# Moving background work, one scatter and 24 transposes in a fused attention, expert and dense kernel

## Chip, core and metric

The kernel runs on one core of a Trainium2 chip. The metric is device time in microseconds (us): the median of three runs of the kernel before is 793.03 us (792.22 to 793.25). The core has TensorE (PE: matmuls, and PEld: its weight loads), VectorE (DVE), ScalarE (ACT), GpSimd (POOL) and SyncE (SP), which issues most transfers. Each engine works through its own instructions in the order in which the program gives them.

## The reference

Attention over a window of 128 with a bias by distance, an expert layer that sends each token to its best of 8 experts, and a dense layer with a squared ReLU. What follows concerns the end of the expert layer and the dense layer.

```python
def reference(**kwargs):
    attn_out = _attn_ref(q, k, v)                      # 4 x 8 x 576 x 64
    x = attn_out.transpose(0, 2, 1, 3).reshape(2304, 512)
    # expert layer: e = argmax of the logits of a token
    #   out = gate * (relu(x @ w1[e]) @ w2[e])         # 512 -> 1024 -> 512
    x = _moe_ref(x=x, **moe_kwargs)
    h = x @ w_in                                       # 512 -> 2048
    r = np.maximum(h, 0.0)
    g = r * r
    return (g @ w_out).astype(np.float32)              # 2048 -> 512
```

All matmuls that matter are done in pairs of numbers: a value is split into a high half and the rest (the low half), and high x high, high x low and low x high are added up. A split is a cast on ScalarE (high) and a subtraction on VectorE or GpSimd (low).

## The kernel before

**Expert stage (up to L1080).** Tokens are gathered into five slots, four of 512 and a last one of 384 (three tiles of 128). A slot has eight up products (`ffn1`, split by `relu_split`) and then, tile by tile, 24 matmuls down (`ffn2`), an eviction and a scatter of the tile's rows to the buffer `yd` in DRAM (`put`: a ScalarE copy and `scatter`, an indirect DMA on GpSimd). In the last slot the third tile is left over. Behind the slots stands a loop (`tc.For_i`, L1106) for tokens that found no slot; its number of turns is read at run time, and in the run shown it is none. After it, `yload(0)` loads the rows of the first dense block on SyncE (it has to wait for the scatters into `yd`), the last slot's third tile is computed, and the rows of the first block are turned so that features lie on partitions: eight groups of three 128x128 pieces, each a matmul with the identity, onto which two 384-column matmuls add what the third tile brings (L1346 to L1353).

**Dense stage.** The hidden features are cut into 4 passes (`PASSES`), the tokens into 3 blocks of 768 (`NB`): 12 visits (`visits`), back and forth over the blocks. A visit has a way up and a way down. `way_up` is a fast matrix product with seven products instead of eight; I number them 1 to 7. A product has two halves of six matmuls of 384 columns. The PSUM banks are three pairs: products 1, 3, 5 and 7 add into the first pair, 2 and 6 into the second, 4 has the third. Between them ScalarE copies the results of products 1 to 3 out (L1263), and VectorE adds those to the results of products 4 to 6 (L1266) and squares them (L1242). So product 3 can't start before the copy of product 1, product 5 not before that of product 3, and product 7 not before VectorE's adds of product 5. `squared` and `split_late` make the halves: a cast on ScalarE (L1234), the low half on GpSimd (L1235). `way_down` has six tiles: the first half of tiles 3, 4, 5, the second half of the same with their eviction (`down_end`, VectorE L1302 from the second pass on, then a store to `ya` on SyncE), and tiles 0, 1, 2 whole. While a visit runs, SyncE loads the next block's operands (`reload`, 768 KB after each product) and earlier sums (`down_load`).

**Background work.** `bg` is a list of generators, and `tick` runs the next step of the first of them. Ticks are called in `way_up` and `way_down` (and in the last expert slot); the instructions of a step enter the queues of their engines there. Three kinds of work run so:
- `weights(p)` (L794): loads two tiles of w_in for pass p, makes four sums (GpSimd) and seven splits of 512 columns, loads two tiles of w_out and splits them (1024 columns). It has 17 steps; the load of w_out is the tenth. `weights(0)` runs in the last expert slot, `weights(1)` from the third visit of pass 0 on, `weights(p+1)` from the second visit of passes 1 and 2 on.
- `late_convs` (L783): four conversions of 64-bit weights, from the first visit of passes 1 and 2 on, in six steps each: load (512 KB); nothing; a ScalarE multiply (L635) and a VectorE mask (L636); a VectorE step (L638); another (L640); a VectorE step (L642) and a GpSimd add (L643). The next step stores the result and issues the next conversion's load.
- `prepare` (operands of the next block) is stepped by itself and is not changed.

Of the kernel before, what the change touches and what calls it, by code (L numbers as in the profile page):

```python
# [24 lines left out]
NSLOT = 5  # L25
MAXSLOT = 12
SHORT = 384
# [25 lines left out]
def attention_moe_kernel(ctx, tc, qh, kh, v, mid, wg, mb, w1, w2, win, wout, out):  # L53
# [740 lines left out]
    def weights(p):  # L794
# [15 lines left out]

        top, low = load(2 * p), load(2 * p + 1)
        yield
        yield
        yield
        yield
        a11, a12, a21, a22 = top[:, :512], top[:, 512:], low[:, :512], low[:, 512:]
        split("a11", a11)
# [10 lines left out]
        s4 = both(a12, s2, ALU.subtract)  # L828
        split("s2", s2)
        yield  # L830
        r = [load(2 * p + 8 + i) for i in range(2)]
        split("a22", a22)
        yield
        split("s4", s4)
        yield
        yield
        for i in range(2):
            h, l = wt("left", F32R), wt("left", F32R)
# [195 lines left out]
    for s in range(NSLOT):  # L1034
# [33 lines left out]
        for i in range(n // 128):  # L1068
            advance_load(8 * s + 4 + i + LA + 1)
            if not nxt and i == n // 128 - 1:  # L1070
                break
            c = slice(128 * i, 128 * i + 128)
            ps = bank("t")
            for f in range(8):
                ffn2(ps, hs[f][0][:, c], hs[f][1][:, c], W[s, 4 + f // 2], f, f == 0, f == 7)
                if f == 4 and 128 * i < nn and nxt:
                    turn(s + 1, i, xr[s + 1][1][i], "v", nn)
                if f == 1 or f == 5:
                    flush()
                    conv_pace(16 * s + 8 + 2 * i + f // 4)  # L1080
                if not nxt and f % 2 == 0:
                    tick()
            put(s, i, ps)
            advance_split(8 * s + 4 + i + LA + (0 if nxt else 1))

    conv_step(EARLY + 1)
# [4 lines left out]
    for s in range(NSLOT - 1):  # L1091
        del xr[s]
        for j in range(8):
            del W[s, j]
    p = ps = None
    held.append({})

# [33 lines left out]
        put("d", 0, ps)  # L1131
    held.clear()
    del xr["d"], xT["d"]
    yload(0)

    s, i = NSLOT - 1, SHORT // 128 - 1
    ids, hot = sm.tile([128, 1], F32, tag="ids", name="ids", bufs=1), wt("left", F32R)
    dve.tensor_copy(ids, xr[s][0][:, i:i + 1])  # L1138
    dve.tensor_tensor(ids, ids, again, op=ALU.add)
# [110 lines left out]
    def way_up(p, ahead, after):  # L1250
# [3 lines left out]
        for n, (o, wo, ps, first) in enumerate((("b11", "a11", a, True), ("t1", "s1", x, True), ("t2", "s2", a, False), ("b21", "a12", z, True), ("t3", "s3", a, False), ("b22", "s4", x, False), ("t4", "a22", a, False))):  # L1254
# [3 lines left out]
            for q in range(2):  # L1258
# [8 lines left out]
                    squared((n == 4, q, n != 3), c)  # L1267
                else:
                    squared((True, q, False), part(), ps[q])
                if q or p == 0:  # L1270
                    tick()
            after(n)
        split_late()

# [36 lines left out]
    def way_down(j, p, between):  # L1311
# [9 lines left out]
        for n, i in enumerate((3, 4, 5)):  # L1321
            ps[i] = bank("vvt"[n])
            products(i, [(True, 0), (True, 1)], True, False)
            tick()
        for i in (3, 4, 5):
            products(i, [(False, 0), (False, 1)], False, True)
            down_end(j, p, i, ps[i])
            between()
            tick()
        for n, i in enumerate((0, 1, 2)):  # L1330
            ps[i] = bank("tvv"[n])
            products(i, [(False, 0), (False, 1), (True, 0), (True, 1)], True, True)
            down_end(j, p, i, ps[i])
            between()
            tick()
        gs.clear()

    def step(n):
# [7 lines left out]
    for n, (k, h) in enumerate(((0, 0), (0, 1), (1, 1), (1, 0))):  # L1346
        for c in range(2):
            p = bank("xmssvvxm"[2 * n + c])[:, :HT]
            m = slice(128 * (2 * k + c), 128 * (2 * k + c) + 128)
            for r in range(3):  # L1350
                pe.matmul(p[:, 128 * r:128 * r + 128], yrow(0, 3 * h + r)[:, m], ident, start=r == 0, stop=False, skip_group_check=True)
            passes(p, [(yhl[:, 512 * b_ + m.start:512 * b_ + m.stop], hot[:, HT * h:HT * h + HT]) for b_ in range(2)], False, True, skip_group_check=True)
            act.copy(raw[k, h][:, c, :], p)  # L1353
        step((2, 1, 3, 1)[n])
# [4 lines left out]
    for n_, (p, j) in enumerate(visits):  # L1359
# [12 lines left out]
            if kept:  # L1372
                reload(visits[n_ + 1][1], n)

        if n_ % NB == (1 if p else 2) and p + 1 < PASSES:
            bg.append(weights(p + 1))
        if n_ % NB == 0 and 0 < p < PASSES - 1:
            bg.append(late_convs(EARLY + LATE * (p - 1)))
        way_up(p, ahead, after)
        between = lambda: None  # L1380
        if fresh is not None:
# [57 lines left out]
```

## Time and profile before

| what | value |
| --- | --- |
| median of three runs | 793.03 us |
| the profiled execution | 790.08 us, span 788.4 us |
| TensorE busy (matmuls) | 744.9 us, 94% of the span |
| TensorE weight loads | 636.0 us, 81% |
| VectorE, ScalarE, GpSimd | 504.0, 342.6, 300.8 us |
| granted clock of TensorE, mean | 0.987 |
| DMA | 174.72 MB, 222 GB/s |

TensorE is busy nearly throughout, so what is read below is where it is not, where its clock is lower, and which engine ends each such wait. The expert stage ends at about 360 us, the dense stage runs from 381.6 us to the end. In a row of the timeline stand: start, length (us), engine, line, operation, output<-inputs, shapes, the number of instructions run together, and in brackets the idle time before the first of them with what ended it. "SPq" and the like are issues of transfers.

### The profile page before, as it was taken

Reading aid. Unit: us, or ns where it says so; the run is one execution under the profiler, and the core shown is the slowest. Engines: PE = TensorE matmul, PEld = TensorE weight load, DVE = VectorE, ACT = ScalarE, POOL = GpSimd, SP = SyncE. Lnnn points to the kernel's source line nnn. Section 1 sums busy time; section 2 is a strip of 40 time slices with the busy share of each in tenths; the row PEclk is TensorE's granted clock in tenths of the full one; section 3 lists DMA queues with packets and bytes.
Section 4 is the critical chain, followed back from the end, with each engine's and each line's share of the span. In section 5 each row is a group of like instructions: output and inputs, shape, how many; then the busy total and the mean of one; then the engine's idle time right before and its main releaser. Section 6 shows DMA issues by size and latency. Waiting matters only on the chain.

```text
span 788.4 us, 12648 instructions
## 1 busy us (share of the span) xinstructions
PE 744.9 (94%) x4207; PEld 636.0 (81%) x4207; DVE 504.0 (64%) x1274; ACT 342.6 (43%) x833; POOL 300.8 (38%) x322
## 2 busy tenths in 40 slices
PE   9999987999999999997989979999999999999997
PEld 7777766777888888895969767978989789898896
DVE  7788889789677768591655436447575475642542
ACT  6676675236345444460655735314332243331230
POOL 4322355022642533441334425235452363540431
PEclk9999999999999999998999997999999999999999
DMA  8567440349776976733668471779827898286832
GB/s 273 172 223 221 141 168 27 121 135 347 241 266 215 319 231 234 267 137 108 228 243 343 183 284 41 291 274 341 303 102 295 277 359 293 95 301 229 338 120 81
DMA packets 71155, 174.72 MB, mean 222 GB/s; under 512 B 10032, under 2 KB 18480, under 8 KB 71088
## 3 DMA queue, kind: packets, MB, share of 16 engines
q1 hardware_dynamic: 68048, 163.93, 58.4%
q0 software_dynamic: 3040, 9.96, 3.3%
q8 instruction: 34, 0.56, 0.3%
q14 instruction: 33, 0.27, 0.1%
HBM read 117.76 MB, written 56.10 MB: 221 GB/s over the span
## 4 chain that ended last, share of the span: by engine, by line
PE 39%; DMA 5%; DVE 4%; issue 3%; POOL 2%; ACT 1%; SPq 0%; POOLq 0%; DVEq 0%; ACTq 0%
PE v L691 14%; PE t L691 10%; PE s L691 9%; PE x L691 2%; PE m L691 2%; DMA w<-wout 2%; DMA w<-win 1%; DVE cr L1242 1%; POOL row L643 1%; DVE cr L1266 1%; DMA w<-wc 1%; POOL hd L1235 1%; DVE w L803 1%; DMA yd<-row,idx 0%; DMA wc<-row 0%
## 5 line engine op out<-in xcount | busy, mean ns | idle before, releaser
L1235 POOL TENSOR_TENSOR hd<-cr,hd 128x384 fp32r<-128x384 f32 x96 | 119.1, 1267 | 144.8 <-ACT hd L1234 137.3
L691 PE MATMUL v<-w,hd 128*128 128x512 f32 x576 | 141.3, 395 | 5.3 <-POOL hd L1235 2.7
L691 PEld LDWEIGHTS v<-w,hd 128*128 128x128 f32 x576 | 107.9, 189 | 32.0 <-POOL hd L1235 6.1
L691 PE MATMUL s<-xq,w 128*128 128x384 f32 x576 | 111.1, 340 | 8.0 <-DVE cr L1266 6.2
L691 PEld LDWEIGHTS s<-xq,w 128*128 128x128 f32 x576 | 102.2, 191 | 11.0 <-DVE cr L1266 7.0
L691 PE MATMUL t<-w,h 128*128 128x512 f32 x408 | 100.6, 400 | 5.6 <-DVE ids L1138 5.6
L691 PEld LDWEIGHTS t<-w,h 128*128 128x128 f32 x408 | 76.3, 191 | 22.2 <-issue 6.0
L643 POOL TENSOR_TENSOR row<-row 128x512 int32<-128x512 int32 x32 | 46.9, 1465 | 117.4 <-DVE row L642 80.2
L1234 ACT CAST hd<-cr 128x384 fp32r<-128x384 f32 x96 | 49.1, 513 | 72.4 <-DVE cr L1242 67.0
L691 PE MATMUL t<-w,hd 128*128 128x512 f32 x288 | 69.2, 389 | 0.0
L691 PE MATMUL s<-w 128*128 128x512 f32 (+1 forms) x292 | 67.9, 384 | 1.1 <-DVE h L716 1.1
L300 ACT ACTIVATE e<-x,m 128x128 f32<-128x128 f32 x128 | 50.3, 396 | 30.2 <-DVE m L279 30.2
L691 PEld LDWEIGHTS t<-w,hd 128*128 128x128 f32 x288 | 54.1, 188 | 11.3
L691 PEld LDWEIGHTS s<-w 128*128 128x128 f32 x292 | 53.3, 188 | 11.3 <-DVE h L716 2.0
L621 DVE TENSOR_TENSOR w<-w 128x1024 fp32r<-128x1024 f32 x37 | 50.0, 1356 | 17.7 <-ACT w L617 17.2
L1263 ACT COPY cr<-s 128x384 f32<-128x384 f32 x48 | 22.6, 479 | 73.4 <-PE s L691 73.4
L1242 DVE SCALAR_TENSOR_TENSOR cr<-cr 128x384 f32<-128x384 f32 x72 | 51.8, 720 | 2.5
L339 POOL TENSOR_SCALAR_AFFINE_SELECT pt<-pt 128x512 f32<-128x512 f32 (+1 forms) x32 | 19.1, 597 | 81.0 <-ACT pt L335 62.0
L1302 DVE SCALAR_TENSOR_TENSOR row<-v,gate,row 128x512 f32<-128x512 f32 x36 | 26.8, 747 | 34.8 <-PE v L691 32.0
L636 DVE TENSOR_SCALAR row<-w 128x512 int32<-128x512 int32 x32 | 13.7, 428 | 46.4 <-DMA w<-win 22.2
L617 ACT CAST w<-w 128x1024 fp32r<-128x1024 f32 x37 | 38.6, 1047 | 2.9 <-DMA w<-w 2.9
L635 ACT ACTIVATE row<-w 128x512 f32<-128x512 f32 x32 | 21.5, 671 | 41.0 <-DMA w<-win 19.4
(293 smaller groups left out, 1360.2 us busy)
## 6 DMA issues: line engine op xcount, KB each, us to landing
xq<-xs SPq DMA_DIRECT2D x42, 768.0 KB
w<-w SPq DMA_DIRECT2D x40, 512.0 KB
xs<-xq SPq DMA_DIRECT2D x21, 768.0 KB
ya<-row SPq DMA_DIRECT2D x54, 256.0 KB
row<-ya SPq DMA_DIRECT2D x54, 256.0 KB
w<-win SPq DMA_DIRECT2D x16, 512.0 KB
wc<-row SPq DMA_DIRECT2D x32, 256.0 KB
w<-wout SPq DMA_DIRECT2D x16, 512.0 KB
```

What stands on the lines that cost most here:

```text
L300: act.activation(e[:, i, j, :], x[:, i, j, :], AF.Exp, bias=m[:, i, j:j + 1], scale=-1.0, accum_out=rinv[b, t][:, h:h + 1])
L339: pool.affine_select(out=diag, in_=prev[:diag.shape[0]], pattern=[[0, 2], [0, 2], [1, n]], channel_multiplier=-1, compare_op=ALU.is_ge, **kw)
L617: (dve.tensor_copy if quick else act.copy)(h, r)
L621: (eng or dve).tensor_tensor(l[:, c], r[:, c], h[:, c].bitcast(F32), op=ALU.subtract)
L635: act.mul(f, hi.bitcast(F32), 2.0 ** -112)
L643: pool.tensor_tensor(a, a, r, op=ALU.add)
L691: pe.matmul(ps, l, r, start=first and i == 0, stop=last and i == n - 1, **kw)
L1234: act.copy(gh, c)
L1235: pool.tensor_tensor(gl, c, gh.bitcast(F32), op=ALU.subtract)
L1242: dve.scalar_tensor_tensor(c, c, 0.0, c, op0=ALU.max, op1=ALU.mult)
L1263: act.copy(c, ps[q])
L1302: dve.scalar_tensor_tensor(o, ps, gate, o, op0=ALU.mult, op1=ALU.add)
```

## The change

It moves work and drops none of it but the second instruction of each turned piece:
- `weights`: the load of w_out is the second step instead of the tenth, and three empty steps go, so that it has 14 steps.
- The first step of `weights(p + 1)`, the load of w_in, is run ahead of the second visit of a pass, in pass 0 too; in pass 0 the rest joins `bg` at the third visit as before.
- `way_up` calls ticks in products 1 to 3 alone: in each half one, in pass 0 two in products 1 and 2. It had one per product (two in pass 0).
- `way_down` calls three ticks after each of tiles 0, 1, 2. It had one after each of its nine parts.
- The second tile of the last expert slot is evicted and scattered behind the loop, ahead of `yload(0)`.
- The 24 pieces of the first block are turned as transposes.

```diff
@@ weights @@
         top, low = load(2 * p), load(2 * p + 1)
         yield
-        yield
-        yield
+        r = [load(2 * p + 8 + i) for i in range(2)]
         yield
...
         split("s2", s2)
         yield
-        r = [load(2 * p + 8 + i) for i in range(2)]
         split("a22", a22)
         yield
         split("s4", s4)
-        yield
         yield
@@ last expert slot and loop @@
-            put(s, i, ps)
+            if nxt or not i:
+                put(s, i, ps)
...
+    ps_ = ps
     p = ps = None
     held.append({})
...
     del xr["d"], xT["d"]
+    s, i = NSLOT - 1, SHORT // 128 - 1
+    put(s, i - 1, ps_)
     yload(0)
@@ way_up @@
-                if q or p == 0:
-                    tick()
+                if n < 3:
+                    tick(2 if p == 0 and n < 2 else 1)
@@ way_down @@
             products(i, [(True, 0), (True, 1)], True, False)
-            tick()
         for i in (3, 4, 5):
             products(i, [(False, 0), (False, 1)], False, True)
             down_end(j, p, i, ps[i])
             between()
-            tick()
         for n, i in enumerate((0, 1, 2)):
...
             between()
-            tick()
+            tick(3)
@@ first block @@
-                pe.matmul(..., ident, start=r == 0, stop=False, skip_group_check=True)
+                pe.matmul(..., ident, is_transpose=True, start=r == 0, stop=False, skip_group_check=True)
@@ visits @@
-        if n_ % NB == (1 if p else 2) and p + 1 < PASSES:
-            bg.append(weights(p + 1))
...
+        if n_ % NB == 1 and p + 1 < PASSES:
+            g = weights(p + 1)
+            next(g)
+            if p:
+                bg.append(g)
+        if p == 0 and n_ == 2:
+            bg.append(g)
         way_up(p, ahead, after)
```

## Rows read from the trace of the kernel before

**Rows 1.** Windows by visit: length; PE, PEld, DVE, ACT, POOL busy; clock; DMA.

```profile
419.30:454.40 35.10, 34.21 (x181) 30.62 (x180) 17.66 (x24) 20.12 (x41) 14.01 (x10) 1.00 0.64 247
454.40:496.56 42.16, 34.85 (x157) 30.59 (x156) 19.61 (x24) 17.41 (x31) 15.16 (x12) 0.88 0.40 155
496.56:529.69 33.13, 31.86 (x157) 27.87 (x156) 17.50 (x27) 9.72 (x19) 12.14 (x10) 1.00 0.84 299
529.69:563.12 33.43, 31.50 (x157) 27.94 (x156) 18.60 (x29) 9.64 (x20) 14.42 (x12) 1.00 0.92 344
563.12:594.82 31.70, 31.43 (x158) 27.97 (x156) 21.26 (x28) 12.22 (x24) 15.65 (x11) 1.00 0.38 138
594.82:627.38 32.56, 31.85 (x157) 27.86 (x156) 18.26 (x28) 9.01 (x18) 12.16 (x10) 1.00 0.85 304
627.38:659.74 32.36, 31.49 (x157) 27.94 (x156) 18.21 (x29) 9.26 (x19) 12.88 (x11) 1.00 0.95 349
...
691.42:722.36 30.94, 30.94 (x157) 28.10 (x156) 12.71 (x20) 7.66 (x16) 9.35 (x8) 1.00 0.77 281
```

**Rows 2.** Timeline of TensorE in an undisturbed visit: products 3 and 7, tiles 1, 2.

```profile
695.60 2.24 PE L691 MATMUL s<-xq,w 128*128 128x384 f32 x12
...
703.92 2.24 PE L691 MATMUL s<-xq,w 128*128 128x384 f32 x12
...
716.92 5.60 PE L691 MATMUL v<-w,hd 128*128 128x512 f32 x24
```

**Rows 3.** Timeline of the third visit: weights' load, first copy, products 5 and 7.

```profile
458.10 3.87 SPq L797 DMA_DIRECT2D w<-wc  x4
...
464.70 0.62 ACT L802 CAST w<-w 128x512 fp32r<-128x512 f32 x1 [4.34 <-DMA w<-wc]
...
465.75 1.34 PE L691 MATMUL s<-xq,w 128*128 128x384 f32 x6 [1.80 <-ACT cr L1263]
...
473.84 2.29 PE L691 MATMUL s<-xq,w 128*128 128x384 f32 x6 [4.67 <-DVE cr L1266]
```

**Rows 4.** Timeline of the last expert slot: two tiles, VectorE's last subtracts.

```profile
348.41 11.44 PE L691 MATMUL t<-w,h 128*128 128x512 f32 x48
...
353.72 2.35 DVE L841 TENSOR_TENSOR w<-w 128x1024 fp32r<-128x1024 f32 x2
```

**Rows 5.** Timeline behind the loop: row loads, last tile, first turned pieces.

```profile
364.74 1.59 SPq L1025 DMA_DIRECT2D w<-yd  x3
...
365.41 7.35 PE L691 MATMUL t<-w,h 128*128 128x512 f32 x24 [5.55 <-DVE ids L1138]
...
372.60 0.83 PE L1351 MATMUL x<-ident,w 128*128 128x128 f32 x6
```

**Rows 6.** Chain that ended last: start, length (us), what; the scatter.

```profile
360.75 3.07 DMA yd<-row,idx
```

**Rows 7.** Transfers from 354 to 375 us, in 40 equal slices.

```profile
GB/s 0 0 0 0 0 0 164 336 0 0 0 0 0 31 0 101 367 31 0 0 0 16 86 246 343 254 269 328 269 218 386 394 168 35 0 0 16 0 0 0
```

**Rows 8.** Timeline of the second visit: four transposes.

```profile
433.89 0.60 PE L1282 MATMUL x<-ident,w 128*128 128x128 f32 x4
```

**Rows 9.** Timeline of pass 1's first two visits: conversions (L635, L636, L628).

```profile
502.62 0.43 DVE L636 TENSOR_SCALAR row<-w 128x512 int32<-128x512 int32 x1 [14.38 <-DMA w<-win]
504.14 0.56 DVE L1266 TENSOR_TENSOR cr<-t,cr 128x384 f32<-128x384 f32 x1 [1.09 <-ACT row L635]
...
527.17 0.75 DVE L1302 SCALAR_TENSOR_TENSOR row<-v,gate,row 128x512 f32<-128x512 f32 x1 [0.22 <-PE v L691]
527.40 0.44 SPq L628 DMA_DIRECT2D w<-win  x1
532.46 0.68 ACT L635 ACTIVATE row<-w 128x512 f32<-128x512 f32 x1 [9.55 <-DMA w<-win]
...
537.23 0.44 SPq L628 DMA_DIRECT2D w<-win  x1
...
545.38 0.43 DVE L636 TENSOR_SCALAR row<-w 128x512 int32<-128x512 int32 x1 [3.32 <-DMA w<-win]
```

## Prediction made before the changed kernel was run

> **What bounds the kernel now.** I read the page first (TensorE busy 94% of 788.4 us, so only its idle time and its clock can be won), then the windows of the dense stage, one window per visit, then the timeline where a window is too long. [Rows 1] give eight of the twelve visits. One in which nothing disturbs TensorE takes 30.94 us, the first of the last pass. The second and third visit of the first pass take 35.10 (it holds 24 transposes) and 42.16 at a granted clock of 0.88; the six middle visits take 31.7 to 33.4. So the work for later weights costs 11.2 us in the third visit and some 9 us in the six after it, and the reader is to see in the rows below who waits for whom there. Inside an undisturbed visit product 3 starts 4.18 us after the visit's start, product 7 12.50 us after it, and tiles 1 and 2 of the way down 25.50 us after it [rows 2].
>
> **Third visit, the weights' load.** Its load is issued 3.70 us into the visit, behind the stores of the visit before; the first ScalarE copy that needs it stands in line until 464.70, and product 5 waits for the ScalarE copy queued behind it (1.80 us); then VectorE is late by the whole of the splits (4.67 and 0.84), and the clock is at its lower level of 1.2 GHz when TensorE returns, six matmuls in 2.29 us instead of 1.34 [rows 3]. After: the first two tiles are loaded a visit earlier, so all seven splits can run beside products 1 to 3, in which VectorE has nothing else. What still loads here is w_out, at the place in SyncE's queue where the first load stands now, so I let it land at the same time, 464.65 (10.25 into the visit). Its ScalarE copy is the tenth step, ahead of the copy of product 3's second half. ScalarE: 1.05 for the tenth step and 0.48 for that copy, so product 5's second half starts at 466.3 instead of 463.8 (454.40 + 4.18 + 2 x 2.08 + 1.04): 2.5 lost. VectorE then does the 1.2 us subtract, two pairs of add and square at 1.1 each and an add, so product 7's halves start 0.5 and 0.3 late; the last low half on GpSimd adds 0.5. Visit: 30.95 + 3.8 = 34.75, **7.4 us won**. Ends: 5.4 if the load lands 2 us later, 11.2 if it lands early enough to hide. The price of the earlier load, 1 MB ahead of the second visit's three row loads on SyncE's queue, is 2.7 us at 390 GB/s, the upper values of a strip [rows 7]; the row loads are read some 14 us after they are issued, so I put it at nothing, up to 2 us if that cover were gone.
>
> **Expert stage, first weights.** The same generator runs for pass 0 beside the last expert slot, and its steps now come two to three ticks sooner. VectorE is full there, up to the two 1.2 us subtracts that stand behind the last hidden tile's low half [rows 4]. One of the two now stands ahead of it. The tiles' matmuls start at 348.41 [rows 4] at 0.227 us each (24 in 5.60 with the tail [rows 2]), so the first tile's last third is due at about 353.6, and the low half is ready at 353.8 now. **1.05 us lost**; between 0 (GpSimd contention shrinks) and 2.4 (both subtracts ahead).
>
> **Scatter behind the loop.** TensorE ends the second-last tile at 359.85 and starts the last one at 365.41 [rows 4, 5]. The chain of waits has the scatter between: it lands at 363.82 [rows 6], and only then do the engines leave the loop's entry, 1.59 us before TensorE starts. Without the scatter ahead of it, the exchange at the entry needs 0.5 to 1.5 us (not shown alone; ends 0 and the 3.97 that it takes now) and the 1.59: TensorE starts at 362.4, 3.0 sooner. But the row loads now stand behind the way out of the entry (1.2; SyncE needs 0.92 now), the copy (0.9 from the tile's end to the scatter's start) and the scatter's 3.07: they leave at 360.85 + 5.2 = 366.0 instead of 364.74 [rows 5, 6]. Their data run until about 371.5 now [rows 7], so until 372.8 then, the first two thirds until 370.9. So the next bound is the row load: the turned pieces start at 370.9 instead of 372.60.
>
> **Pieces turned.** A piece is two instructions now, three pieces in 0.83 us [rows 5]; a transposed one is one instruction, four in 0.60 [rows 8]; the difference gives 0.115 per instruction, 24 times less: 2.7 us. Groups of three pieces and two 384-column matmuls shrink from 1.02 to 0.68. Eight groups from 370.9, with 0.5 of waiting for the last row load, end at 377.0 where the first visit now starts at 381.6. Both edits together: **4.6 us won**, from 2.7 (only the pieces) to 6.0 (the row loads hidden). A rule speaks against it: the Trainium skill (TensorE: Matmul & The Clock Gate, Part 4: PE-mode transpose) says that transposes don't count as activity for the clock. By it the groups would run at the lower level (rival d); the trace doesn't agree so far, since a visit with 24 transposes holds 1.00 [rows 1].
>
> **Conversions at the end of a way down.** This part decides. In the first two visits of passes 1 and 2 the queue of extra work is four conversions of six steps: load; nothing; ScalarE multiply and VectorE mask, which wait for the load; two VectorE steps; a VectorE step and a GpSimd add; then the store and the next load. The first fits the six ticks of products 1 to 3: it lands 6.06 into the visit [rows 9], ScalarE still finishes product 3's first copy at 7.7 to 8.2, and product 5 needs it at 8.3. So the first visits lose nothing: 31.0 for 33.13 and 32.56, **-3.6 us**.
>
> The second conversion is loaded after tile 0. VectorE's eviction (0.75) is followed by the tile's store and, 0.8 behind it, by the conversion's load [rows 9], so 25.5 + 0.2 + 0.75 + 0.75 = 27.2 into the visit. Its mask is in the same tick, ahead of tile 1's eviction. Load to mask is 5.06 in the quiet stretch (527.40 to 532.46), 8.15 beside the reloads (537.23 to 545.38) [rows 9]; I take 5.0, since the reloads are over by then: 1.3 into the next visit. From the mask to the following load it takes 4.77 (532.46 to 537.23, with one eviction in between, as here). So conversion 3 is loaded 6.0 into the second visit, its multiply stands on ScalarE ahead of the copy of product 1, and ends its wait at 11.0. Multiply 0.68, copy 0.48: product 3 starts at 12.2 instead of 4.18, **8.0 lost**. Now the same wait ends 2.8 into the visit and costs nothing [rows 9]. Queued behind the waiting instructions are on VectorE the evictions of tiles 1 and 2, on SyncE their stores and the next reloads; nobody needs those within 8 us.
>
> Conversion 4 is loaded at 11.0 + 4.1 (no eviction between) = 15.1 and lands at 20.1; VectorE's mask stands ahead of product 4's add. Mask 0.43, four adds and squares at 0.56, an add, 0.2 of handing over [rows 9]: product 7 starts at 23.5. TensorE would be there at 12.2 + 8.32 = 20.5: 3.0 more, and 0.5 for the last low halves on GpSimd. A second visit so takes 30.94 + 11.5 = 42.4, against 33.43 and 32.36: **+19.1 us** for both passes. A lower clock after 8 us without matmuls costs nothing here up to 3 us, as conversion 4 ends later. The third visits get most splits before they start: 31.1 instead of 31.7, **-1.2** for both. For the last pass nothing changes.
>
> **Sum.** 1.05 - 7.4 - 4.6 - 3.6 + 19.1 - 1.2 = +3.35 us. On the profiled execution, 790.1 with a span of 788.4, that is 793.4; the median of the runs shown is 2.95 above it, so **796.4**.
>
> **Rivals.** (a) The end of the way down is cover enough and no conversion reaches TensorE: the second visits take 31.2, -3.4 instead of +19.1; 773.9. For it: ScalarE stands 9.55 us for conversion 3 now and TensorE loses nothing. Against: that wait ends with 1.4 us to spare, and the load moves 8 us back. Chance 0.11. (b) Loads on the quiet queue are shorter: the 256 KB scatter lands in 3.07, and another 256 KB at 390 GB/s make 3.7. Each of three waits shrinks by 1.3, 3.9 per pass: 788.6. This decides the sign below some 4.4 us per load. The Trainium skill (DMA: Bandwidth & Descriptors, Anatomy of one DMA) gives 2.0 us plus bytes over 436 GB/s, an estimate of 3.2 for 512 KB, and by it the time would be 785.6; no conversion's load in this trace is that short. Chance 0.09. (c) Conversions 3 and 4 meet the reloads, as 8.15 shows: 3.1 more each, 12.4 in all, 808.8. Chance 0.07. (d) The clock falls over the transposes: eight groups at 1.2 GHz cost 0.68 each, 5.4 us; 801.8. Chance 0.04. The forecast has 0.69; that the scatter wins nothing (1.9 us) lies within it.
>
> **How the numbers follow.** The forecast's own range is 791.5 to 802: 1.2 us on the loop, 2 on the third visit, 3 on the second visits together. About 0.2% (1.6 us) is what a measurement tells from no change. Of the forecast's 0.69, 0.04 lie below 791.4 and 0.12 within 1.6 us. Faster: 0.11 + 0.06 of (b) + 0.04 = 0.21. Same: 0.12 + 0.02 of (b) = 0.14. Slower: 0.65. The range of 8 in 10 leaves out (a), most of (c) and the forecast's far end: 786 to 804.
>
> **What would show it.** Second visits of passes 1 and 2 at some 42 us with a TensorE gap of 8 us ahead of product 3, released by ScalarE, whose multiply waits for a load; then 3 us ahead of product 7, released by VectorE. Third visit of pass 0 near 35. No scatter ahead of the loop, TensorE off for 2.5 us there and again for 1 to 2 us before the pieces, which have half as many instructions. If the second visits stay near 31, step by step the queue argument is wrong, and (a) holds.

## The result, and the profile after

The changed kernel takes 799.60 us (median of 20 runs, 794.74 to 801.73) where the kernel before takes 794.73 in the same comparison (20 runs, 792.22 to 798.09): ratio 1.0056, 95% interval 1.0041 to 1.0071. It is slower by 4.9 us, clear of the 0.2% that a measurement can't tell. The profiled execution has a span of 798.9 us at a mean granted clock of 0.974, where before had 788.4 and 0.987.

The page's group for the products of the way up tells in one line what happened: 21.3 us of idle time ahead of them, 19.6 of it ended by ScalarE's copies. Before, the same group had 8.0 us, most of it ended by VectorE's adds. Kernel before, then kernel after:

```profile
L691 PE MATMUL s<-xq,w 128*128 128x384 f32 x576 | 111.1, 340 | 8.0 <-DVE cr L1266 6.2
L691 PE MATMUL s<-xq,w 128*128 128x384 f32 x576 | 114.1, 347 | 21.3 <-ACT cr L1263 19.6
```

Windows by visit, kernel after, with the columns of [rows 1]: second and third visit of pass 0, the three visits of pass 1, the first two of pass 2.

```profile
416.88:451.98 35.10, 34.21 (x182) 30.62 (x181) 17.65 (x24) 20.12 (x41) 14.44 (x11) 1.00 0.71 276
451.98:489.54 37.56, 34.03 (x157) 30.87 (x156) 17.68 (x24) 17.14 (x31) 15.47 (x12) 0.91 0.39 146
489.54:521.10 31.56, 31.25 (x158) 27.96 (x157) 14.07 (x22) 8.71 (x18) 10.64 (x9) 1.00 0.83 305
521.10:565.01 43.91, 34.77 (x158) 30.34 (x156) 20.68 (x34) 9.80 (x20) 14.49 (x12) 0.88 0.73 268
565.01:595.96 30.95, 30.95 (x158) 28.10 (x157) 21.22 (x28) 12.38 (x24) 14.35 (x12) 1.00 0.39 142
595.96:627.58 31.62, 31.31 (x157) 27.94 (x156) 14.90 (x23) 8.03 (x17) 10.55 (x9) 1.00 0.82 307
627.58:671.01 43.43, 34.84 (x158) 30.43 (x156) 20.68 (x34) 9.81 (x20) 14.49 (x12) 0.88 0.74 269
```

Against [rows 1]: the second visits of passes 1 and 2 have grown by 10.5 and 11.1 us; all else in the dense stage has shrunk or stayed. The third visit of pass 0 fell from 42.16 to 37.56, the first visits from 33.13 and 32.56 to 31.56 and 31.62, and the third visit of pass 1 is at the 30.95 us of an undisturbed one (that of pass 2 too). The second visit of pass 0 is 35.10 as before, although 1 MB for later weights is now loaded ahead of its row loads.

Timeline of the second visit of pass 1, kernel after (columns as in [rows 9]):

```profile
526.92 0.45 SPq L628 DMA_DIRECT2D w<-win  x1
...
532.85 0.67 ACT L635 ACTIVATE row<-w 128x512 f32<-128x512 f32 x1 [9.87 <-DMA w<-win]
...
533.43 0.84 ACT L1263 COPY cr<-s 128x384 f32<-128x384 f32 x2
...
533.94 4.21 PE L691 MATMUL s<-xq,w 128*128 128x384 f32 x12 [8.50 <-ACT cr L1263]
...
537.09 0.43 SPq L628 DMA_DIRECT2D w<-win  x1
...
542.31 0.43 DVE L636 TENSOR_SCALAR row<-w 128x512 int32<-128x512 int32 x1 [7.04 <-DMA w<-win]
...
545.38 0.79 PE L691 MATMUL s<-xq,w 128*128 128x384 f32 x3 [0.32 <-DVE cr L1266]
```

Read it from the top: conversion 3 is loaded 5.82 us into the visit; ScalarE stands 9.87 us for it; the two copies of product 1 that are queued behind its multiply run at once at 533.43; product 3 starts 0.5 us later, 12.84 us into the visit, after 8.50 us without a matmul. Twelve matmuls that take 2.24 us in [rows 2] then take 4.21. Conversion 4 comes by the same road, but at product 7 only 0.32 us of idle time is left of it. The windows of this visit show why product 3 is slow: TensorE's clock is at its lower level of 1.2 GHz from 529.19, while TensorE idles, to 539.43. The third line is the same stretch in the second visit of pass 2, where product 3 starts after 7.56 us without a matmul.

```profile
521.10:529.19 8.09, 4.35 (x25) 4.02 (x23) 3.46 (x6) 0.69 (x1) 1.26 (x1) 1.00 0.45 136
529.19:539.43 10.24, 5.49 (x17) 5.49 (x18) 2.24 (x4) 3.13 (x7) 1.27 (x1) 0.50 0.84 286
...
635.00:645.24 10.24, 5.75 (x18) 5.75 (x19) 2.24 (x4) 3.14 (x7) 1.28 (x1) 0.50 0.94 301
```

The last expert slot, the loop and the first turned pieces, TensorE's timeline of the kernel after, to be held against [rows 4, 5]:

```profile
350.36 4.51 PE L691 MATMUL t<-w,h 128*128 128x512 f32 x19
355.80 1.19 PE L691 MATMUL t<-w,h 128*128 128x512 f32 x4 [0.93 <-DVE w L621]
357.40 5.96 PE L691 MATMUL t<-w,h 128*128 128x512 f32 x25 [0.41 <-DVE h L716]
365.44 7.29 PE L691 MATMUL t<-w,h 128*128 128x512 f32 x24 [2.07 <-DVE w L1141]
372.56 0.49 PE L1349 MATMUL x<-ident,w 128*128 128x128 f32 x3
```

The two tiles take 13.0 us (from 350.36 to 363.36) instead of 11.44. TensorE is off for 2.07 us ahead of the last tile instead of 5.55, and the pieces follow the last tile without a wait. The dense stage starts 15.8 us after the second tile's end (379.17 less 363.36) instead of 21.7.

### The profile page after: what moved, and what is told of

Its sections match the earlier page's. It is cut to its first block, busy times and chain, and to the rows that moved or that the text cites. A ratio compares the mean times of both kernels' runs of the same rounds, so it can differ in the third digit from the quotient of the medians.

```text
span 798.9 us, 12612 instructions
## 1 busy us (share of the span) xinstructions
PE 748.9 (94%) x4183; PEld 640.9 (80%) x4183; DVE 500.6 (63%) x1274; ACT 341.2 (43%) x833; POOL 294.7 (37%) x322
## 5 line engine op out<-in xcount | busy, mean ns | idle before, releaser
L1235 POOL TENSOR_TENSOR hd<-cr,hd 128x384 fp32r<-128x384 f32 x96 | 112.5, 1207 | 113.6 <-ACT hd L1234 113.5
L691 PE MATMUL v<-w,hd 128*128 128x512 f32 x576 | 138.7, 391 | 1.3 <-POOL hd L1235 1.3
L691 PE MATMUL s<-xq,w 128*128 128x384 f32 x576 | 114.1, 347 | 21.3 <-ACT cr L1263 19.6
L691 PEld LDWEIGHTS s<-xq,w 128*128 128x128 f32 x576 | 104.9, 195 | 24.9 <-ACT cr L1263 20.5
L621 DVE TENSOR_TENSOR w<-w 128x1024 fp32r<-128x1024 f32 x37 | 49.6, 1344 | 17.3 <-ACT w L617 17.3
L1242 DVE SCALAR_TENSOR_TENSOR cr<-cr 128x384 f32<-128x384 f32 x72 | 53.9, 749 | 2.5
L635 ACT ACTIVATE row<-w 128x512 f32<-128x512 f32 x32 | 21.5, 672 | 63.6 <-DMA w<-win 34.2
L636 DVE TENSOR_SCALAR row<-w 128x512 int32<-128x512 int32 x32 | 13.6, 426 | 52.3 <-DMA w<-win 28.2
```

Source lines behind the costliest of these rows:

```text
L621: (eng or dve).tensor_tensor(l[:, c], r[:, c], h[:, c].bitcast(F32), op=ALU.subtract)
L635: act.mul(f, hi.bitcast(F32), 2.0 ** -112)
L691: pe.matmul(ps, l, r, start=first and i == 0, stop=last and i == n - 1, **kw)
L1235: pool.tensor_tensor(gl, c, gh.bitcast(F32), op=ALU.subtract)
L1242: dve.scalar_tensor_tensor(c, c, 0.0, c, op0=ALU.max, op1=ALU.mult)
```

## The experiments

Each is the kernel before or the kernel after with one edit; one has two (it adds its edit to that of the run ahead of it) and the last has three. "Ratio" is against the kernel before on the same chip. The kernel before has medians of 791.73 to 794.73 us in these comparisons, so ratios are compared, not times.

**The kernel before once more.** No edit.

> The kernel before once more, for a second profile. The profiled execution of before (790.1 us) lies under all of its other runs (792 to 798), and the changed stretches of the two traces differ by +8.6 us where the medians differ by +4.9. Theory: the visits of the dense stage repeat within 0.3 us (35.1, 42.2, 33.1, 33.4, 31.7, 32.6, 32.4, 31.7, 30.9) and what varies is the clock in the attention stage, so the last expert slot's tiles start 1 to 4 us later than at 348.4. Rival: the dense stage of before varies, above all the third visit (42.2) or the second visits, whose load's wait ends with 1.4 us to spare; then a visit there is 2 to 5 us longer.

Measured: 792.98 us, span 791.3. Windows of three of its visits: the third of pass 0, the second of passes 1 and 2.

```profile
455.10:497.90 42.80, 35.20 (x157) 30.82 (x156) 19.60 (x24) 17.42 (x31) 15.19 (x12) 0.88 0.40 152
...
530.87:564.63 33.76, 31.59 (x158) 27.90 (x156) 18.61 (x29) 9.68 (x20) 14.47 (x12) 1.00 0.93 342
629.67:662.60 32.93, 31.50 (x157) 27.95 (x156) 18.60 (x29) 9.26 (x19) 13.46 (x11) 1.00 0.93 344
```

Against [rows 1] a visit repeats within 0.8 us (the largest difference is the first visit of pass 2, 33.37 for 32.56), so the 10 us of the second visits are the change's. The span is 2.9 us longer than in the execution the prediction started from. The theory put such a difference into the attention stage, and that does not hold: the last slot's tiles start at 348.33 (348.41 in the other execution), and what is longer lies behind them, in the last tile (8.28 us for 7.35) and, 0.3 to 0.8 us each, in four visits of the dense stage.

**The calls for background work as before.** Everything else of the change stays.

```diff
@@ way_up @@
-                if n < 3:
-                    tick(2 if p == 0 and n < 2 else 1)
+                if q or p == 0:
+                    tick()
@@ way_down @@
             products(i, [(True, 0), (True, 1)], True, False)
+            tick()
...
             between()
+            tick()
...
-            tick(3)
+            tick()
```

> The changed kernel with the ticks of the kernel before (one per product and one per part of the way down); loads, scatter and turned pieces stay as changed. Theory (queue): the second visits of passes 1 and 2 return from 43.9 and 43.4 to 33.4 and 32.4 us, the first and third visits lose their 1.6, 0.9, 0.7 and 0.7 again, and the third visit of pass 0 gets shorter by some 3, since the split of w_out no longer stands ahead of a copy: 799.6 - 21.5 + 3.9 - 3 = 779 us. Rival (work): the same work costs the same wherever it stands and the time stays within 3 us of 799.6.

Measured: 784.07 us, ratio 0.9905 (0.9872 to 0.9937). The placing of the calls alone is worth 12 us against the kernel after, and without it the change would have been faster. It came out 5 us above what the theory gave, and the windows of the second visits of passes 1 and 2 show where (the third visit of pass 0 takes 32.84 us):

```profile
514.79:552.05 37.26, 32.96 (x157) 28.89 (x156) 22.31 (x33) 11.98 (x24) 19.00 (x14) 0.95 0.92 341
616.50:653.16 36.66, 33.23 (x157) 29.09 (x156) 22.86 (x33) 11.97 (x24) 19.02 (x14) 0.95 0.92 340
```

The second visits are 37, not the 33 of before. Their timeline shows conversion 4 behind the early load of the next weights:

```profile
519.12 0.92 SPq L797 DMA_DIRECT2D w<-wc  x2
...
523.04 0.43 SPq L628 DMA_DIRECT2D w<-win  x1
...
533.35 0.43 DVE L636 TENSOR_SCALAR row<-w 128x512 int32<-128x512 int32 x1 [6.19 <-DMA w<-win]
...
534.48 4.11 PE L691 MATMUL v<-w,hd 128*128 128x512 f32 x9 [4.25 <-ACT hd L1234]
```

From load to mask it takes 10.31 us, 8.15 before [rows 9], and the way down waits 4.25 us for casts queued on ScalarE behind the multiply.

**The same without the early load in passes 1 and 2.**

```diff
             g = weights(p + 1)
-            next(g)
             if p:
                 bg.append(g)
+            else:
+                next(g)
```

> The changed kernel with the calls for background work of the kernel before (as in the run with those calls) and, besides, without the early load of the next weights in passes 1 and 2: there the whole generator joins the list at the second visit, as in the kernel before. Theory: in the run with the calls of before the second visits (37.26 and 36.66 against 33.43 and 32.36) were longer because the early 1 MB stands ahead of the fourth conversion's load on SyncE's queue and in the transfers: load to mask 10.3 us there, 8.15 before. Without it 8.2 us again, second visits of 33.4 and 32.6, and 784.07 - 7.9 = 776 us. Rival: the longer second visits come from the shorter generator (its first steps meet the conversions sooner), not from the load: they stay near 37, 784 us.

Measured: 778.70 us, where the theory had 776; ratio 0.9838 (0.9796 to 0.9880). Load to mask (522.54 to 530.75) is 8.21 us again, and the second visits (pass 1, pass 2) come most or all of the way back:

```profile
515.03:549.99 34.96, 33.02 (x157) 29.04 (x156) 18.86 (x30) 10.94 (x22) 16.36 (x13) 0.95 0.92 347
614.77:647.69 32.92, 31.72 (x157) 27.90 (x156) 17.10 (x27) 9.59 (x20) 14.41 (x12) 1.00 0.93 346
```

So the early load has a price, but who pays depends on what stands behind it: nothing waits for the row loads behind it in pass 0 (35.10 us before and after), but TensorE, by way of ScalarE's casts, waits for a conversion's load behind it.

**All four conversion loads in the first step**, the calls left as the change has them.

```diff
         for key, i in convs[k:k + LATE]:
             conv_load(key, i)
+        for key, i in convs[k:k + LATE]:
             yield
```

> The changed kernel with all four loads of the late conversions issued in their first step; the steps themselves, and where they stand, stay as changed. Theory (queue): ScalarE's multiply no longer waits for a load, so the gap of 8 to 9 us ahead of product 3 goes, with the lower clock behind it; the second visits take 31.5 us: 799.6 - 24.3 = 775 us. Rival (work): the bunch of steps at the end of a way down and in products 1 to 3 is itself what delays the way up; the second visits stay above 40 us and the time above 795.

Measured: 773.05 us, ratio 0.975 (0.9722 to 0.9778). Windows: third visit of pass 0, second visits of passes 1 and 2.

```profile
452.94:488.40 35.46, 32.26 (x158) 27.83 (x156) 17.71 (x24) 17.10 (x31) 15.50 (x12) 1.00 0.41 155
519.71:550.66 30.95, 30.95 (x158) 28.10 (x156) 18.41 (x30) 8.74 (x18) 14.62 (x12) 1.00 0.88 334
612.68:643.63 30.95, 30.95 (x157) 28.10 (x156) 18.42 (x30) 8.74 (x18) 14.63 (x12) 1.00 0.88 334
```

All instructions but the loads stand in the same places, and the second visits are undisturbed. It is the waits for the loads that cost, not the work of the conversions: this decides for the prediction's queue argument and against the rival of this run.

**Conversion 4 alone loaded with the first**, to price its wait apart.

```diff
-        for key, i in convs[k:k + LATE]:
-            conv_load(key, i)
+        for n, (key, i) in enumerate(convs[k:k + LATE]):
+            if n < LATE - 1:
+                conv_load(key, i)
+            if n == 0:
+                conv_load(*convs[k + LATE - 1])
```

> The changed kernel, but the fourth conversion of passes 1 and 2 is loaded together with the first, so that no load of its own stands ahead of its mask in the second visits; the waits for the second and third are left. Theory from the trace of the changed kernel: the fourth conversion's wait is hidden there already, because TensorE comes back from the third conversion's wait at its lower clock and reaches product 7 late anyhow; the second visits go from 43.9 and 43.4 to about 43 (the 0.3 and 1.0 us ahead of product 7 go), the time to about 798.5. Rival (the prediction's term): the wait ahead of product 7 was worth 3.0 us a visit besides the clock: second visits of 40.6, the time 793.6.

Measured: 796.25 us, ratio 1.0021 (1.0004 to 1.0038): 0.35 points, 2.8 us, below the kernel after. Second visits of passes 1 and 2, the stretches at the lower clock in each, and last the third visit of pass 0, which the edit doesn't touch:

```profile
522.78:564.86 42.08, 33.86 (x157) 30.70 (x156) 20.70 (x34) 9.71 (x20) 14.56 (x12) 0.88 0.72 268
627.44:668.30 40.86, 33.05 (x158) 29.88 (x156) 20.70 (x34) 9.70 (x20) 14.57 (x12) 0.92 0.73 274
...
530.87:541.11 10.24, 5.76 (x18) 5.76 (x19) 2.58 (x5) 3.72 (x8) 1.33 (x1) 0.50 0.84 283
636.69:643.51 6.82, 3.91 (x12) 3.91 (x13) 2.58 (x5) 2.66 (x6) 1.33 (x1) 0.50 0.88 346
...
454.76:491.22 36.46, 32.80 (x158) 29.63 (x156) 17.70 (x24) 17.10 (x31) 15.51 (x12) 0.95 0.40 151
```

Neither theory holds as written. The two visits are 1.8 and 2.6 us shorter than in the trace of the kernel after, between the 0.3 and 0.7 that stand ahead of product 7 there and the 3.0 of the prediction. Two things had escaped me. VectorE's late adds pace product 7 and what follows as well: from product 7 to the visit's end pass 1 takes 19.6 us in the kernel after (545.38 to 565.01), 18.4 here. And in pass 2 the stretch at the lower clock is 6.82 us long where the kernel after has 10.24: 3.91 us of matmuls at that level instead of 5.75, so 0.9 of the 2.6 us is the clock and not conversion 4.

**w_out for pass 1 loaded a visit earlier as well.**

```diff
         top, low = load(2 * p), load(2 * p + 1)
+        if p == 1:
+            r = [load(2 * p + 8 + i) for i in range(2)]
         yield
-        r = [load(2 * p + 8 + i) for i in range(2)]
+        if p != 1:
+            r = [load(2 * p + 8 + i) for i in range(2)]
```

> The changed kernel with w_out of pass 1 loaded together with w_in, a visit earlier. Theory: the third visit of pass 0 (37.6 us; 3.5 of it product 5 waiting for the ScalarE copy behind the split of w_out, and some 3 at the lower clock after it) takes 31.2 us: 793 us. Rival: the seven splits in products 1 to 3 are too dense for ScalarE and VectorE in any case, and the visit stays above 35 us, the time above 797.

Measured: 796.05 us, ratio 1.0041 (1.0020 to 1.0063), where the theory had 793. Second and third visit of pass 0:

```profile
415.86:452.00 36.14, 34.16 (x181) 30.60 (x180) 17.65 (x24) 20.39 (x41) 14.38 (x11) 1.00 0.76 297
452.00:484.52 32.52, 31.94 (x158) 27.87 (x157) 17.61 (x24) 17.01 (x31) 15.50 (x12) 1.00 0.35 137
```

The third visit is 5.0 us shorter than in the trace of the kernel after, so the rival (it stays above 35) falls; the theory had 31.2. But 1.0 comes back in the second visit, where the row loads now stand behind 2 MB and a transpose waits for them:

```profile
432.24 0.63 PE L1285 MATMUL x<-ident,w 128*128 128x128 f32 x4 [1.64 <-DMA w<-yd]
```

In the trace another 1.5 us goes in the first visit (39.23 us at a clock of 0.96, where the kernel after has 37.71 at 1.00), and 1.6 in the second visits. No edit touches the first visit; the same lower clock in it stands in two other runs (loads ahead, conversion 4 ahead). The times give 1.2 us against the kernel after, so of the 5 us little is left, and I count it as a win of the visit, not of the kernel.

**The calls as before in pass 0 alone.**

```diff
-                if n < 3:
-                    tick(2 if p == 0 and n < 2 else 1)
+                if n < 3 or p == 0:
+                    tick()
...
             products(i, [(True, 0), (True, 1)], True, False)
+            tick(p == 0)
...
             between()
+            tick(p == 0)
...
-            tick(3)
+            tick(3 if p else 1)
```

> The changed kernel with the calls for background work of the kernel before in pass 0 alone. Theory: in the third visit of pass 0 it is the crowding of the calls into products 1 to 3 that puts w_out's split on ScalarE ahead of the copy of product 3's second half; spread over the whole visit the split comes later, the load is in by then, no wait and no fall of the clock: third visit 32.8 instead of 37.56, 799.6 - 4.7 = 794.9 us, and the second visits of passes 1 and 2 stay near 43.5. Rival: the load of w_out is late because of where it stands in SyncE's queue, so something waits for it in either order: third visit 35 to 37.5 and 797 to 800 us.

Measured: 794.84 us, ratio 1.0037 (1.0014 to 1.0061). The third visit is 32.86 at a clock of 1.00:

```profile
448.25:481.11 32.86, 31.80 (x157) 27.86 (x156) 18.36 (x24) 17.38 (x31) 16.20 (x12) 1.00 0.44 167
```

The load of w_out leaves at the same place, 4.19 us into the visit (4.16 in the kernel after). What changed is the order on ScalarE: the first split of w_out now comes 11.8 us into the visit, and waits for nothing. So with the load in the same place a later split takes the wait away, and in the run ahead of this one, with the calls crowded as they are, an earlier load does: what counts is the distance between the two. In the times the gain is smaller than in the visit: 0.19 points of ratio, 1.5 us, with intervals of some 1 to 2 us to either side; the 4.7 us are shown by this pair of traces, not by the ratio. (The second visits of passes 1 and 2, which the edit leaves alone, take 44.91 and 42.97 here.)

**The first weights' steps as before in the last expert slot.**

```diff
         yield
-        r = [load(2 * p + 8 + i) for i in range(2)]
+        if p:
+            r = [load(2 * p + 8 + i) for i in range(2)]
+        else:
+            yield
+            yield
...
+        if p == 0:
+            r = [load(2 * p + 8 + i) for i in range(2)]
         split("a22", a22)
...
+        if p == 0:
+            yield
```

> The changed kernel, but weights(0) in the last expert slot has its steps where the kernel before has them (its load of w_out again the tenth step, the empty steps back). Theory: the two tiles down take 11.4 us from first to last matmul again instead of 13.0, and nothing else moves: 799.6 - 1.6 = 798.0 us. Rival: the later splits delay the last tile behind the loop or the first pieces by as much, so the dense stage starts 15.8 + 1.6 us behind the second tile's end and the time stays at 799.6.

Measured: 796.80 us, ratio 1.0046 (1.0018 to 1.0073). The two tiles take 11.4 us again, one row without a wait; the window below it is the third visit of pass 0:

```profile
350.61 11.41 PE L691 MATMUL t<-w,h 128*128 128x512 f32 x48
...
449.45:484.84 35.39, 32.62 (x158) 29.32 (x156) 17.71 (x24) 17.10 (x31) 15.52 (x12) 0.95 0.41 155
```

That is the 1.6 us of the theory in the trace; in the ratio 0.1 points, 0.8 us, too little to tell from none. The dense stage starts 14.6 us behind the second tile's end (376.65 less 362.02), so the rival falls.

The third visit of pass 0 has the same instructions here as in the kernel after and is 2.2 us shorter. In the four traces with this visit as the change has it, it takes 37.56 (kernel after), 36.46 (conversion 4 ahead), 35.46 (loads ahead) and 35.39 us. A gain in it read from one pair of traces is uncertain by as much.

**The scatter behind the loop alone**, in the kernel before.

```diff
-            put(s, i, ps)
+            if nxt or not i:
+                put(s, i, ps)
...
+    s, i = NSLOT - 1, SHORT // 128 - 1
+    put(s, i - 1, ps_)
     yload(0)
```

> The kernel before with one part of the change alone: the second-last tile is evicted and scattered behind the loop. Theory: the scatter ahead of the loop's entry cost TensorE the difference between the idle time of before (5.55 us) and that of the changed kernel (2.07 us) ahead of the last tile, and the row loads that now start later are still in time for the first turned piece, as in the changed kernel: 3.5 us won, so 789.1 us where before has 792.6, with TensorE idle for about 2.1 us ahead of the last tile and nothing ahead of the first piece. Rival (the prediction's bound): the pieces wait for the row loads, 1.5 to 2 us of idle time ahead of the first piece, 1.9 us won: 790.7. If the loop's entry costs the same with no scatter ahead of it: 792.6.

Measured: 789.21 us, ratio 0.9934 (0.9909 to 0.9959): 5.2 us won, where the theory had 3.5. TensorE's timeline:

```profile
363.00 5.78 PE L691 MATMUL t<-w,h 128*128 128x512 f32 x24 [2.14 <-DVE w L1144]
...
370.01 0.49 PE L1354 MATMUL x<-ident,w 128*128 128x128 f32 x2 [0.63 <-DMA w<-yd]
```

2.14 us of idle time instead of 5.55. Besides, the last tile runs in 5.78 us where [rows 5] have 7.35: after this stop the clock stayed up. That is 1.6 us which no step of the prediction had. Now that the tile is quick, the row loads are seen: the first group waits 0.63 us for them.

**The pieces turned as transposes alone**, in the kernel before.

```diff
-                pe.matmul(..., ident, start=r == 0, stop=False, skip_group_check=True)
+                pe.matmul(..., ident, is_transpose=True, start=r == 0, stop=False, skip_group_check=True)
```

> The kernel before with one part of the change alone: the 24 pieces of the first block are turned as transposes. Theory: 24 instructions less at 0.115 us each, a group of three pieces in 0.49 instead of 0.83 us and no fall of the granted clock over the eight groups: 2.7 us won, 789.9 us where before has 792.6. Rival (transposes do not count as activity, so the clock falls over the groups): the granted clock at its lower level over the groups, 384-column matmuls at twice their time there, up to 5.4 us lost against 2.7 won: 795.3.

Measured: 791.97 us, ratio 0.9971 (0.9953 to 0.9990): 2.3 us won, by the interval 0.8 to 3.7. Windows of its last tile and of the eight groups:

```profile
366.30:374.22 7.92, 7.92 (x25) 6.25 (x26) 1.43 (x8) 0.00 (x0) 0.00 (x0) 0.69 0.60 200
374.22:380.82 6.60, 5.97 (x41) 5.25 (x40) 3.16 (x4) 5.17 (x10) 0.97 (x1) 1.00 0.22 87
```

The clock was at its lower level in part of the tile ahead (0.69 in the mean), rose, and stays at 1.00 over the groups, in which 24 transposes stand among 16 matmuls of 384 columns.

**Three edits together**: all conversion loads ahead, the calls as before in pass 0 alone, the first weights' steps as before. The lines are those of the three experiments above:

```diff
+        for key, i in convs[k:k + LATE]:
             yield
...
+        if p == 0:
+            r = [load(2 * p + 8 + i) for i in range(2)]
         split("a22", a22)
...
+                if n < 3 or p == 0:
+                    tick()
...
+            tick(3 if p else 1)
```

> The changed kernel with three things set by what the runs showed: all four loads of the conversions at once in the first step, the calls for background work of the kernel before in pass 0 alone, and the steps of the first weights in the last expert slot where the kernel before has them. Theory: the second visits of passes 1 and 2 at 31.0 as in the run with the loads ahead, the third visit of pass 0 at 32.8 as in the run with the calls of before (2.6 us less than 35.45), 1.5 us less in the last expert slot: 773.05 - 2.6 - 1.5 = 769 us. Rival: the third visit is set by when w_out is loaded and not by which calls there are, so it stays at 35.5 and the time is 771.5.

Measured: 768.09 us, ratio 0.966 (0.9630 to 0.9689), span 767.2. Third visit of pass 0 and second visit of pass 1, and the page's group for the products of the way up:

```profile
450.56:483.40 32.84, 31.78 (x157) 27.84 (x156) 18.36 (x24) 17.37 (x31) 16.20 (x12) 1.00 0.44 167
515.05:546.00 30.95, 30.95 (x158) 28.10 (x156) 18.42 (x30) 8.75 (x18) 14.61 (x12) 1.00 0.88 334
```

```profile
L691 PE MATMUL s<-xq,w 128*128 128x384 f32 x576 | 108.4, 335 | 0.9 <-DVE cr L1275 0.7
```

Faster than both kernels, 1 us below what was expected, and the products have 0.9 us of idle time ahead of them where the kernel after has 21.3. The rival on the third visit (35.5) falls.

## Why the prediction came out, step by step

The forecast was 3.35 us slower, 796.4; measured are 4.9 slower and 799.6, inside the range. The mechanism of the large term was the predicted one, but several terms were off and partly cancel, so that the total came as near as it did is in part luck. By the traces of the kernel before and after, and in brackets against the second profile of before, the terms are:

| term | predicted | traces (second profile) |
| --- | --- | --- |
| last expert slot | +1.05 | +1.56 (+1.6) |
| scatter and turned pieces | -4.6 | -5.9 (-6.8) |
| third visit of pass 0 | -7.4 | -4.6 (-5.2) |
| first visits, passes 1 and 2 | -3.6 | -2.5 (-3.2) |
| second visits | +19.1 | +21.6 (+20.7) |
| third visits | -1.2 | -1.5 (-1.5) |
| sum | +3.35 | +8.6 (+5.6) |

The sum from the profile that I used lies 3.7 us above the measured 4.9. The two executions differ by more than the medians do, 10.5 us (790.08 and 800.59): that of before is quicker than each of the 20 runs timed beside the kernel after, that of after is 1 us above its median. Against the second profile the sum fits within 0.8, but a visit that no edit touches differs by up to 2.2 us between executions, so such a fit proves little.

**Second visits: right in place, road and nearly in size.** Conversion 2's mask was put 1.3 us into the visit (measured 1.14); conversion 3's load at 6.0 (measured 5.82), the end of its wait at 11.0 (11.75), product 3 at 12.2 (12.84). Load to end of wait is 5.9 us for conversion 3 and 5.2 for conversion 4 (526.92 to 532.85, 537.09 to 542.31) in pass 1, 5.0 and 5.4 in pass 2, where I took 5.0. The step that failed is the last one, that a lower clock after 8 us without matmuls costs nothing because conversion 4 ends later. Both cost. With conversion 4's wait taken away the visit of pass 1 is still 2.9 above what the 8.22 of wait in that run explain (42.08 less 30.95 less 8.22), and half of the 5.76 us that TensorE worked at its lower clock is 2.9. In the kernel after the visits split the same way: 43.91 is 30.95, 8.50 of wait for conversion 3, 2.7 for the clock (half of 5.49) and a rest of 1.7; 43.43 is 30.95, 7.56, 2.9 (half of 5.75) and a rest of 2.0. That rest is what conversion 4 cost. I had 0 for the clock and 3.5 for conversion 4. In three other runs with the same second visits (w_out earlier, calls of pass 0, first weights) they take 44.9 to 45.3 and 43.0 to 44.0 us.

**Third visit: right sign, mis-sized by 2.2 to 2.8 in this trace.** Two things, both in this timeline of the kernel after:

```profile
456.14 2.50 SPq L797 DMA_DIRECT2D w<-wc  x2
...
463.58 1.04 ACT L836 CAST w<-w 128x1024 fp32r<-128x1024 f32 x1 [4.38 <-DMA w<-wc]
464.53 0.47 ACT L1263 COPY cr<-s 128x384 f32<-128x384 f32 x1
...
465.06 2.29 PE L691 MATMUL s<-xq,w 128*128 128x384 f32 x6 [3.53 <-ACT cr L1263]
```

The chain (split waits for w_out, the copy of product 3's second half stands behind it, product 5 waits) is the predicted one. But the load lands 11.6 us into the visit, not 10.25, so 3.53 us are lost ahead of product 5 and not 2.5; and after that stop product 5 runs at the lower clock (six matmuls in 2.29 us; the visit's clock is 0.91). The lower clock stood in [rows 3] behind a longer stop, and I let it go with that stop. Neither is the same in every execution: in the run with the loads ahead, whose third visit is the same, the load lands 10.9 us into the visit, 2.80 us are lost and the clock is 1.00 throughout, and its 35.46 us are 0.7 above the 34.75 that I had. The experiment with the calls of before in pass 0 shows a cure: let the split come when the load is in.

**Loop and pieces: won more than said, one step wrong.** The pieces are as sized (0.68 a group, 2.3 us by the ratio against 2.7). The row loads did not leave 6.15 us behind the second tile's end but 4.2 (367.56 to 363.36, in the other run 3.9): I had let 2.2 us pass for the loop's entry and the way out of it ahead of the eviction's copy, and ScalarE starts that copy 0.34 us behind the tile's end (363.70). So the row loads delay TensorE by nothing here, and by 0.6 to 1.0 us in the runs in which the last tile runs at the full clock. The scatter alone won 5.2 us by its ratio, with an interval from 3.3 to 7.2, against the 1.9 left for it in the sum.

**Last expert slot:** One of VectorE's 1.2 us subtracts does stand ahead of the hidden tile's low half (L716, the wait of 0.41). An earlier wait of 0.93 is for the low half of an expert weight (L621), which VectorE also reaches later; the working had no such term. In all 1.56. The working's own figures (ready at 353.8, due at 353.6, 1.2 later) give 1.2 more than now, not 1.05.

**The early load at nothing:** true in pass 0, where the second visit has 35.10 before and after. It wasn't true in general. With 2 MB ahead of the row loads 1.0 us shows in the second visit; and with the calls of before in passes 1 and 2, the 1 MB ahead of conversion 4 costs 2.3 and 3.7 us a visit (37.26 to 34.96, 36.66 to 32.92). In the kernel after it stands behind conversion 3's load in those passes; no run prices it there.

**The rivals.** (a), that the end of a way down is cover enough, falls with the 8.5 us. (b), shorter loads, falls with 5.0 to 5.9 us for 512 KB. The fit in the Trainium skill (DMA: Bandwidth & Descriptors, Anatomy of one DMA), by which 512 KB are estimated at 3.2 us, is given there for transfers that GpSimd issues. These loads are issued by SyncE, on a queue that also carries stores and reloads, and take longer; the measurement decides. (c), a clash with the reloads, isn't seen in the kernel after (5.0 to 5.9 where the clash in [rows 9] has 8.15). (d) falls: from 368.76 on the clock is 1.00 over all groups, and in the run with that edit alone too. The rule of the Trainium skill (TensorE: Matmul & The Clock Gate, Part 4: PE-mode transpose), that transposes don't count as activity, isn't refuted by this, since matmuls stand between them; but no cost follows from it in a mix of this kind.

**What stays open.** Whether the clock falls after the loop's entry: the last tile takes 7.29 to 7.37 us in the traces of three kernels (the kernel after, w_out earlier, conversion 4 ahead) and 5.73 to 5.78 in those of seven others with the same 2.1 us of idle time ahead of it. No run here tells what decides, nor why the third visit of pass 0 takes anything from 35.39 to 37.56 us with the same instructions. The 4.7 us won there in one pair of traces is 2.5 against the shortest of these, which is nearer to the 1.5 of the ratio.

## What to carry to other kernels

Where background work is fed into in-order queues, place the issue of each load apart from the instruction that waits for it: the same conversions at the same calls cost some 12.5 to 13 us a visit (43.91 and 43.43 less 30.95) with each load issued two calls ahead of its use, and nothing with all loads issued at the start. Before calls are moved to a stretch that seems idle, ask of every step that waits what stands behind it in its engine's queue in the new place, and when that is due. A load that is moved ahead is free only as long as what is queued behind it has slack.

## What was not expected of the hardware

A stop of 8.5 us cost some 11 us. In both second visits of the kernel after the clock fell to 1.2 GHz while TensorE stood still, and was still there when it came back: 5.49 us of matmuls ran at that level in pass 1, half of which is lost, so the price of the wait is 8.5 and another 2.7. After the 3.53 us stop of the third visit the clock was low too (six matmuls in 2.29 us). After shorter stops it was low in some executions and not in others: at 1.00 throughout the third visit with a stop of 2.80 us, and low in some last tiles behind a stop of 2.1 us. I had taken the price of a stop to be the stop.
